# RWKV-7 recurrence with a GELU feed-forward layer: first loads in half transfers

## The chip, the cores and the metric

One core of a Trainium2 chip. The core has five engines that run side by side, each in the order of its own program: PE (matmuls), DVE (vector work), ACT (activations and copies), POOL (a slower vector engine) and SP, which here only issues DMA transfers. 16 DMA engines move the data. The metric is the device time of one execution in microseconds; before and after are compared by their medians.

## The reference

Inputs are r, k, v, w, a, b of shape batch 4, heads 8, 768 time steps, 40 per head, and two weights. Each head keeps a 40x40 state:

```python
for t in range(S):
    y[:, :, t] = einsum('bhd,bhde->bhe', r_t, state)
    Sa = einsum('bhde,bhe->bhd', state, a_t)
    state = state * w_t[:, :, None, :] - einsum('bhd,bhe->bhde', Sa, b_t) \
            + einsum('bhd,bhe->bhde', v_t, k_t)
...
x = y.transpose(0, 2, 1, 3).reshape(3072, 320)
h = x @ w_in                      # 320 x 2048
out = (0.5 * h * (1 + erf(h / sqrt(2)))) @ w_out
```

All inputs arrive at this kernel as written, and the two weights in 8-byte words (`wide_in`, `wide_out`), which the kernel has to turn to 4-byte floats itself.

## The kernel before

Time is cut into 12 chunks of 64 steps. In a chunk the recurrence is a set of small matmuls over 32 (batch, head) pairs. Its results go, 256 tokens at a time, through the feed-forward layer, one chunk behind.

Every piece of work is a named step, a small Python function. `order()` (line 19) is one long list of step names with their arguments, written out by hand; line 1436 performs them in that order. Each engine receives its instructions in the order in which the steps come, and does not reorder ACT, DVE, POOL or SP work. So a wait on ACT holds up everything that stands behind it on ACT. Waits are put in by the tile framework where a tile is read after it is written. Each DMA transfer has one of eight completion semaphores, taken in turn.

The steps that matter here, with their lines:

- Row loads, all issued by SP. `Lw.c` (472), `La.c` (483), `Lb.c` (490), `Lk.c` (494) and, for the first chunks, `Lr.c` (508) call `load_rows` (458), which brings chunk c of one input, 64 time steps by 16 (batch, head) rows of 40 floats for each half e of the partitions. Each run in memory is 160 bytes. From chunk 3 on, `Lw`, `La` and `Lr` load in another way (`load_pairs`, line 463, and line 479); `Lb` and `Lk` keep `load_rows`. `LV` (498) has its own code with the same shape, at line 500.
- Word loads. `Lf.kt.x.part` (544) brings 64 rows of words of w_in, each run 2 KB; where kt is 3 and x is 1 it takes 40 rows and 24 rows. `Lf5` (555) brings the last 16-row pieces (line 561), `Ls` (586) words of w_out (line 591).
- Their readers. `lg.c` (697, instructions at line 699) takes the logarithm of what `Lw.c` brought, on ACT. `ce.u` (621, lines 625 and 626) is the first step of turning unit u of words to floats, on ACT, followed by work on DVE. `ce.2` needs `Lf.2.0.0` and `Lf.2.1.0`; `ce.5` needs `Lf.0.0.1` and `Lf.0.1.1`; `ce.4` needs the `Lf5` words.
- The chain of chunk 0. `qm.k` (990) squares a 32x32 block matrix on PE, `qz.k` (1008) transposes on DVE, `qb.k.z` (1013) masks, one half on ACT (line 1016). Then `vm.0` (895), `jm.0` (1047) and `km.0` (1072) on PE, `jc.0` (1061, line 1065), `qx` (1034, line 1036), `xc0.0` (1135, line 1131) and `kt0.0` (1096, line 1090) on ACT.
- `warm` steps (449) are matmuls whose result nobody reads.

The part of the list around the first loads reads (cut):

```python
... Lw.0 pads_extra.0 Lb.0 ... La.0 ... Lw.1 ... Lf.0.0.0 ... Lf.0.1.0 ... Lb.1 ...
... Lf.1.0.0 ... Lf.2.0.0 ... Lf.1.1.0 ... La.1 ... Lf.3.0.0 ... Lk.0 Lf.3.1.0 ... Lf5.1.0 ...
... Lf.0.1.1 ... Lr.0 Lf.2.1.1 ... LV.0 ... Lf.2.1.0 ... Lf.2.0.1 ... Lk.1 ... Lf.0.0.1 Lw.2 ...
... Lb.2 ... La.2 ... Lf5.0.0 ... LV.1 Ls.4 ... Ls.0 ... Lf5.0.1 ... Lf5.1.1 ...
```

Of the kernel before, what the change touches and what calls it, by code (L numbers as in the profile page):

```python
# [114 lines left out]
def kernel(  # L115
# [13 lines left out]
    B, H, S, D = r.shape  # L129
# [4 lines left out]
    BL = 32  # L134
    NP = H // 2
    G = B // 2
# [10 lines left out]
    NB = 3  # L147
# [9 lines left out]
    def tile_of(name, shape, dtype=FP32):  # L157
        return const.tile(shape, dtype, name=name)
# [25 lines left out]
    def half(j, n=HP):  # L184
        return slice(j * HP, j * HP + n)
# [24 lines left out]
    part = tile_of("part", [P, G, DM])  # L210
# [112 lines left out]
    def engine(queue):  # L323
        return {"s": nc.sync, "a": nc.scalar, "p": nc.gpsimd}[queue]
# [131 lines left out]
    def rows_of(src, c, e):  # L456
        return src[G * e:G * (e + 1), :, c * C:(c + 1) * C, :].rearrange("g h t d -> t (g h) d")

    def load_rows(c, src, t, eng):
        for e in range(2):  # L460
            eng.dma_start(out=t[half(e)].rearrange("p g h d -> p (g h) d")[:, :, :D], in_=rows_of(src, c, e))

    def load_pairs(c, src, t, eng):
        rows = slice(c * C // 2, (c + 1) * C // 2)
# [6 lines left out]
    @step  # L471
    def Lw(c, q="s"):
        to = rows(w_of(c))
        if c < NB:
            load_rows(c, w, to, engine(q))
        else:
            for e in range(2):
                for g in range(G):
                    engine(q).dma_start(out=to[half(e ^ g), g],  # L479
                                        in_=w[G * e + g, :, c * C:(c + 1) * C].rearrange("h t d -> t h d"))  # L480

    @step
    def La(c, q="s"):
        if c < NT:
            load_rows(c, a, by_64(a_of(c)).rearrange("p (g h) d -> p g h d", g=G), engine(q))
        else:
            load_pairs(c, a, paired["a"], engine(q))

    @step
    def Lb(c, q="s"):  # L490
        load_rows(c, b, rows(b_of(c)), engine(q))
# [41 lines left out]
    def first_home(kt, part):  # L533
        if not wide_in:
            return w_in_sb[:, kt, part * LW // 2:(part + 1) * LW // 2]
        if part == 0:
            return flat_out[:, kt * LW:(kt + 1) * LW]
        return flat_xt[:, :LW] if kt == NK - 1 else flat_gt[:, kt * LW:(kt + 1) * LW]
# [4 lines left out]
    @step  # L543
    def Lf(kt, x, part, q="s"):
        words = first_home(kt, part).rearrange("p (b n) -> p b n", b=2)
        src = first_from.rearrange("r (j x n) -> x r j n", x=2, n=FW // 2)[x]
        at, row = x * HP, x * D + 2 * D * kt
        n = min(HP, DM - row)
        for to, begin, many in (at, row, n), (at + n, 0, HP - n):
            if many:  # L550
                engine(q).dma_start(out=words[to:to + many],
                                    in_=src[begin:begin + many, 2 * part:2 * part + 2])

    @step
    def Lf5(part, x, q="s"):
# [912 lines left out]
```

## Time and profile before

| what | value |
|---|---|
| median of 3 runs | 632.1 us (631.37 to 632.44) |
| the profiled execution | 632.67 us |
| its span, first to last instruction | 630.9 us |
| mean granted clock of PE | 0.995 |
| DMA moved | 63.97 MB in 246,550 packets, 101 GB/s |
| HBM read / written | 54.39 MB / 3.93 MB |

In a timeline row stand the start in us from the span's start, the duration, the engine and line, what is written and read, the number of merged instructions, and in brackets how long the engine was idle before and what ended that. `SPq` rows are SP's issues of DMA transfers: their duration is the time of issuing, not of the transfer. A row of a group of issues gives the shortest, median and longest duration in ns and the first and last start. A window row gives busy time and instructions of PE, PEld, DVE, ACT and POOL, then PE's granted clock, the DMA engines' busy share (packets overlap, so it can exceed 1) and GB/s.

### The profile page before, as it was taken

How to read it: one execution, taken by the hardware profiler on the slowest of the kernel's cores; microseconds unless marked ns; L12 is line 12 of the kernel's file. 1: busy time of each engine (PE TensorE's matmuls, PEld its weight loads, DVE VectorE, ACT ScalarE, POOL GpSimd, SP SyncE). 2: the span in 40 equal slices, each digit the busy share in tenths (PEclk: the TensorE clock that was granted, in tenths of full speed). 3: DMA queues.
4: the chain of work that ended last, by engine and by line, in shares of the span. 5: the costliest groups of instructions: out<-in, count | busy, mean ns of one | idle time of the engine just before them, and what ended most of it. 6: DMA issues, size and time to landing. Idle time of an engine off the chain costs nothing.

```text
span 630.9 us, 31485 instructions
## 1 busy us (share of the span) xinstructions
PE 619.7 (98%) x14196; PEld 521.8 (83%) x14196; DVE 454.4 (72%) x558; ACT 345.4 (55%) x475; POOL 369.6 (59%) x797
## 2 busy tenths in 40 slices
PE   8989999999999999999999999999999999999997
PEld 5777787777987987987987988987988978978977
DVE  1788998875979978996886785875867955744313
ACT  4866897685454637636654647445557435243020
POOL 6278565738814875868848818838813886830000
PEclk9998999999999999999999999999999999999999
DMA  9997887722555766665575554444663454110100
GB/s 153 166 155 166 188 181 175 132 62 47 117 109 86 146 116 119 128 124 102 98 133 101 108 108 87 83 77 96 123 132 51 85 87 86 34 25 4 43 3 21
DMA packets 246550, 63.97 MB, mean 101 GB/s; under 512 B 228216, under 2 KB 243328, under 8 KB 246416
## 3 DMA queue, kind: packets, MB, share of 16 engines
q1 hardware_dynamic: 245976, 61.68, 52.0%
q8 instruction: 111, 1.82, 1.2%
q10 hardware_dynamic: 440, 0.29, 0.2%
q14 instruction: 23, 0.19, 0.1%
HBM read 54.39 MB, written 3.93 MB: 92 GB/s over the span
## 4 chain that ended last, share of the span: by engine, by line
PE 95%; ACT 1%; DVE 1%; SPq 1%; issue 1%; DMA 0%; DVEq 0%; ACTq 0%
PE bank L1308 33%; PE bank L188 30%; PE bank L1347 27%; PE bank L1429 3%; PE bank L763 2%; SPq L479 0%; SPq L1226 0%; DMA xt<-xt 0%; ACT st L1016 0%; DVE os L1298 0%; ACT L727 0%; ACT N L918 0%; DVE N L876 0%; ACT kT L727 0%; ACT gt L1313 0%
## 5 line engine op out<-in xcount | busy, mean ns | idle before, releaser
L1308 PE MATMUL bank<-xt,w_in_sb 64*64 64x256 f32 x3840 | 220.5, 377 | 1.1 <-DMA xt<-xt 1.1
L957 POOL TENSOR_TENSOR tmp<-W,Nb 128x126 f32<-128x126 f32 (+22 forms) x341 | 156.9, 460 | 77.3 <-DVE Nb L923 51.7
L1308 PEld LDWEIGHTS bank<-xt,w_in_sb 64*64 64x64 f32 x3840 | 147.1, 133 | 52.1 <-issue 1.8
L959 POOL TENSOR_TENSOR W<-W,tmp 128x126 f32<-128x126 f32 (+22 forms) x341 | 163.7, 480 | 26.7
L1347 PE MATMUL bank<-w_out_sb,gt 128*128 128x160 f32 x704 | 102.0, 302 | 0.2 <-ACT gt L1313 0.2
L1347 PEld LDWEIGHTS bank<-w_out_sb,gt 128*128 128x128 f32 x704 | 96.6, 190 | 3.5 <-issue 1.3
L1313 ACT ACTIVATE gt<-bank 128x1024 f32<-128x1024 f32 x48 | 49.1, 1024 | 73.1 <-PE bank L1308 71.9
L1152 DVE TENSOR_TENSOR SM<-bank,upper 128x832 f32<-128x832 f32 (+1 forms) x24 | 22.9, 989 | 19.5 <-PE bank L188 19.4
L1262 ACT COPY conv<-st 32x128 f32<-32x128 f32 (+2 forms) x55 | 28.0, 510 | 14.5 <-DVE st L1256 13.7
L1298 DVE TENSOR_TENSOR os<-os,bank 128x160 f32<-128x160 f32 x44 | 14.0, 319 | 28.5 <-PE bank L1347 19.1
L1347 PE MATMUL bank<-extra,conv 128*128 128x160 f32 x208 | 30.0, 299 | 0.0
L1313 ACT ACT_TABLE_LOAD x23 | 29.5, 1283 | 0.4
L1298 DVE TENSOR_TENSOR conv<-gt 128x1024 f32<-128x1024 f32 x11 | 14.0, 1272 | 21.0 <-ACT gt L1313 21.0
L1347 PEld LDWEIGHTS bank<-extra,conv 128*128 128x128 f32 x208 | 28.9, 190 | 0.0
L1204 DVE TENSOR_TENSOR st<-bank,st 128x832 f32<-128x832 f32 (+1 forms) x22 | 21.2, 986 | 8.8 <-PE bank L188 8.8
L1347 PE MATMUL bank<-extra,gt 128*128 128x160 f32 x176 | 26.4, 303 | 0.2 <-DVE os L1298 0.2
L734 DVE TENSOR_TENSOR_SCAN kT<-spare,kT 128x256 f32<-128x256 f32 x36 | 26.1, 782 | 0.6 <-ACT kT L727 0.6
L1347 PEld LDWEIGHTS bank<-extra,gt 128*128 128x128 f32 x176 | 24.3, 190 | 1.5 <-issue 0.9
L942 POOL MEMSET W<- 128x512 f32 x11 | 5.8, 525 | 32.9 <-DVE Tt L928 32.9
L801 POOL TENSOR_TENSOR bk_rows<-bk_rows,part 128x640 f32<-128x640 f32 x9 | 14.5, 1614 | 14.1 <-DMA bk_rows<-in_k_dram 14.1
L699 ACT ACT_TABLE_LOAD x11 | 14.1, 1283 | 13.8 <-DMA w_tile<-in_w_dram 13.7
L754 ACT ACT_TABLE_LOAD x11 | 14.1, 1283 | 13.1 <-PE bank L188 12.7
(227 smaller groups left out, 1156.1 us busy)
## 6 DMA issues: line engine op xcount, KB each, us to landing
bk_rows<-in_b_dram SPq DMA_DIRECT2D x24, 160.0 KB
bk_rows<-in_k_dram SPq DMA_DIRECT2D x24, 160.0 KB
out_dram<-os SPq DMA_DIRECT2D x46, 80.0 KB
VR<-in_v_dram SPq DMA_DIRECT2D x22, 160.0 KB
w_tile<-in_w_dram SPq DMA_DIRECT2D x36, 80.0 KB
v_pairs<-in_w_dram SPq DMA_DIRECT2D x18, 144.0 KB
a_pairs<-in_a_dram SPq DMA_DIRECT2D x18, 144.0 KB
a_pairs<-in_b_dram SPq DMA_DIRECT2D x18, 144.0 KB
```

Of the source, the lines that this page charges most:

```text
L188: nc.tensor.matmul(o, lhsT, rhs, start=first, stop=True, skip_group_check=True)
L734: nc.vector.tensor_tensor_scan(logs[:, at:at + n], onward, logs[:, at:at + n], 0.0, ALU.mult, ALU.add)
L957: nc.gpsimd.tensor_tensor(t, W[:, BL // 2 - rows:, rest:rest + 1].to_broadcast([P, rows, rest]), Nb[:, rest:rest + 1, :rest].to_broadcast( ...
L959: nc.gpsimd.tensor_tensor(own, own, t, ALU.add)
L1152: nc.vector.tensor_tensor(SM[:, g, :, :, cols], pair_of(f"S{c}_", g).rearrange("p x i c -> p i x c")[:, :, :, cols], kept, ALU.mult)
L1204: nc.vector.tensor_tensor(to, pair_of(f"QY{c}_", g)[:, :, :, cols], to, ALU.add)
L1262: nc.scalar.copy(apart.rearrange("p e i g d -> p (e i g) d")[to_rows, :, to_col:to_col + n], st.rearrange("p e i g c -> p (e i g) c")[rows ...
L1298: nc.vector.tensor_tensor(to, one_, other, how)
L1308: nc.tensor.matmul(ph[half(x ^ y), x, s], w_in_sb[half(x), kt, at:at + HP], xt[half(x), kt], start=kt == 0, stop=kt == NK - 1, skip_group_ ...
L1313: nc.scalar.activation(gt[:, 4 * q:4 * q + 4].rearrange("p (x s) t -> p x s t", x=2), bank(f"ph{c}_{q}").rearrange("p x (s t) -> p x s t", ...
L1347: nc.tensor.matmul(po[:, n, :DM // 2], l_[:, f], r_[:, f], start=f == 0, stop=f == NF // 2 - 1)
L1429: nc.tensor.matmul(po[:, g, :DM], gt[:, f, g * P:(g + 1) * P], w_out_sb[:, f], start=f == 0, stop=f == NF - 1)
```

## The change

`load_rows` now cuts the transfer of each half e in two, 8 of the 16 (batch, head) rows each, if the chunk is one of the first three (`NB` is 3, `H` is 8, `G` is 2). From chunk 3 on it stays one transfer. `Lf` cuts every piece into parts of at most 32 rows (`BL` is 32): 64 rows become 32 and 32, 40 become 32 and 8, 24 stay. The steps, their list and every other instruction stay; `LV`, `Lf5`, `Ls` and the pair loads are untouched. What waits for a load now waits for all its parts.

```diff
     def load_rows(c, src, t, eng):
         for e in range(2):
-            eng.dma_start(out=t[half(e)].rearrange("p g h d -> p (g h) d")[:, :, :D], in_=rows_of(src, c, e))
+            to, words = t[half(e)].rearrange("p g h d -> p (g h) d")[:, :, :D], rows_of(src, c, e)
+            for n in range(0, G * H, H if c < NB else G * H):
+                some = slice(n, n + H if c < NB else G * H)
+                eng.dma_start(out=to[:, some], in_=words[:, some])
...
         for to, begin, many in (at, row, n), (at + n, 0, HP - n):
-            if many:
-                engine(q).dma_start(out=words[to:to + many],
-                                    in_=src[begin:begin + many, 2 * part:2 * part + 2])
+            for m in range(0, many, BL):
+                k = min(BL, many - m)
+                engine(q).dma_start(out=words[to + m:to + m + k],
+                                    in_=src[begin + m:begin + m + k, 2 * part:2 * part + 2])
```

## The prediction

> **What bounds the kernel now.** I read the page first (busy shares, slices, chain), then the timeline of SP's queue, the early timeline, and the windows.
>
> ```profile
> span 630.9 us, 31485 instructions
> PE 619.7 (98%) x14196; PEld 521.8 (83%) x14196; DVE 454.4 (72%) x558; ACT 345.4 (55%) x475; POOL 369.6 (59%) x797
> ...
> DMA  9997887722555766665575554444663454110100
> ...
> PE 95%; ACT 1%; DVE 1%; SPq 1%; issue 1%; DMA 0%; DVEq 0%; ACTq 0%
> ```
>
> PE is busy 98% and makes 95% of the chain that ended last: what PE loses early it has little idle time to win back. All changed transfers lie in the first 85 us of a 631 us span. There the DMA engines are full: the first three slices read 9.
>
> ```profile
> 4.00:8.00 4.00, 4.00 (x7) 1.61 (x6) 0.00 (x0) 2.70 (x3) 3.67 (x19) 1.00 1.12 171
> 16.00:20.00 4.00, 3.89 (x38) 2.78 (x38) 2.36 (x5) 3.37 (x6) 0.00 (x0) 1.00 1.15 199
> ```
>
> Last two columns: DMA share and GB/s. Row loads (160-byte runs) move at 171 GB/s, words (2 KB runs) at up to 199. Which loads matter shows in the waits, and in the rows right behind a load:
>
> ```profile
> 5.28 1.28 ACT L699 ACT_TABLE_LOAD   x1 [5.28 <-DMA w_tile<-in_w_dram]
> ...
> 38.72 0.77 ACT L625 ACTIVATE conv<-w_out_sb,rebias 128x512 int16<-128x512 int16 x1
> ...
> 39.40 0.77 ACT L626 ACTIVATE conv<-w_out_sb,rebias 128x512 int16<-128x512 int16 x1
> ...
> 40.21 0.72 ACT L1016 ACTIVATE st<-st,of_half 128x512 f32<-128x512 f32 x1
> ...
> 40.99 2.06 PE L188 MATMUL bank<-turned,st 64*64 64x32 f32 x64
> ...
> 46.12 1.28 ACT L699 ACT_TABLE_LOAD   x1 [1.48 <-DMA w_tile<-in_w_dram]
> ...
> 47.42 0.74 ACT L699 ACTIVATE w_tile<-w_tile 128x640 f32<-128x640 f32 x1
> ...
> 48.78 1.18 ACT L1065 COPY turned<-bank 32x512 f32<-32x512 f32 x2 [0.63 <-PE bank L188]
> ...
> 49.98 2.50 ACT L1036 COPY Tt<-turned 32x512 f32<-32x512 f32 x4
> ...
> 52.71 0.85 ACT L1131 COPY SM<-bank 128x832 f32<-128x832 f32 x1 [0.23 <-PE bank L188]
> ...
> 54.66 0.57 ACT L1090 COPY Tt<-bank 32x512 f32<-32x512 f32 x1 [1.09 <-DVE Tt L1090]
> ```
>
> Three places on ACT, which works strictly in its written order. Lw.0 is waited for at 5.28. At 38.72 ACT converts words of Lf.2.1.0 (step ce.2), and right behind it stand qb.3.1.a (40.21) and PE's qm.4 (40.99), which needs it: a microsecond lost at ce.2 is lost by PE. At 46.12 ACT waits 1.48 us for Lw.2, but behind it three waits on others (0.63, 0.23, 1.09) leave 1.95 us before step kt0 at 54.66 moves.
>
> **The change part by part.** It removes no work and moves no step: the same bytes go in more issues. 15 row loads (Lw, La, Lb, Lk, Lr of chunks 0 to 2) go from 2 transfers to 4, which adds 30. 14 word transfers of 64 rows become two of 32, the two of 40 rows become 32 and 8, those of 24 stay: 16 more. So 46 more issues on SP, all between 0.8 us and 85 us. What does one cost?
>
> ```profile
> L461 SPq DMA_DIRECT2D bk_rows<-in_b_dram x24: 595/674/2370, 2.3 to 506.5; - x24
> ...
> L479 SPq DMA_DIRECT2D w_tile<-in_w_dram x36: 595/633/1767, 107.9 to 533.3; - x36
> ...
> L551 SPq DMA_DIRECT2D w_out_sb<-in_moe_w_in_dram x9: 299/1091/2581, 8.2 to 32.6; - x9
> ...
> L469 SPq DMA_DIRECT2D v_pairs<-in_w_dram x36: 312/488/1699, 86.7 to 473.0; - x36
> ...
> L561 SPq DMA_DIRECT2D w_out_sb<-in_moe_w_in_dram x8: 422/444/2811, 46.6 to 56.6; - x8
> ```
>
> (ns, shortest/median/longest.) L479 is already the new row transfer's shape: 64 partitions of 8 heads of 40. It takes 0.633 us, and its shortest, 0.595, is that of L461 with 16 heads. So an issue costs the same for half the bytes. For 32 rows of words there is no row. Below it stands L561 (16 rows, 0.422), above it a 64-row one:
>
> ```profile
> 34.05 0.61 SPq L551 DMA_DIRECT2D gt<-in_moe_w_in_dram  x1
> ```
>
> I take L469's 0.488, since it too has 32 partitions, and keep 0.422 and 0.61 as bounds. Between issues lies 0.04 us (0.81+1.46 to 2.31):
>
> ```profile
> 0.81 1.46 SPq L461 DMA_DIRECT2D w_tile<-in_w_dram  x2
> 2.31 1.70 SPq L461 DMA_DIRECT2D bk_rows<-in_b_dram  x2
> ...
> 26.26 0.61 SPq L551 DMA_DIRECT2D gt<-in_moe_w_in_dram  x1
> 27.37 1.32 SPq L461 DMA_DIRECT2D r_pairs<-in_r_dram  x2
> ...
> 31.20 1.32 SPq L500 DMA_DIRECT2D VR<-in_v_dram  x2
> 32.57 1.44 SPq L551 DMA_DIRECT2D w_out_sb<-in_moe_w_in_dram  x1
> ...
> 39.92 1.31 SPq L461 DMA_DIRECT2D w_tile<-in_w_dram  x2
> ```
>
> A half row transfer is 82 KB, 0.48 us at 171 GB/s, against 0.67 us of SP: SP becomes slower than the engines on rows. A half word transfer is 131 KB, 0.66 us at 199 GB/s, against 0.53: there the engines still set the pace.
>
> The Trainium skill, DMA: Bandwidth & Descriptors, section Issuing engines are not separate DMA queues, says that the sequencer's time to initiate a DMA is usually small relative to the DMA. By that the change would cost nothing; the L479 row speaks against it here.
>
> Now SP's clock, unstalled. Up to the end of Lf.2.1.0: start 0.81; 8 row loads, 32 issues of 0.67, 21.5; words 9x2+3 = 21 of 0.53, 11.1; four L561 of 0.48, 1.9; one VR, 1.4; the 0.5 us hole before 27.37. Sum 37.2, against 32.57+1.44 = 34.0 before. From end of issue to landing: Lw.0 ended its issue at 2.27 and ended a wait at 5.28, 3.0 us with an almost empty queue; Lw.2, 41.23 to 46.12, 4.9 us with a full one. When SP is the slower side the queue is short, so I take 3.0: ce.2's words land at 40.2, against ACT's 38.72. That is **+1.5 us** at ce.2, and through qb.3.1.a at PE's qm.4. With 0.422 for the words it is 38.8, +0.1; with 0.61, 42.8, about +4.
>
> Lw.2: two more row loads and two word transfers in halves, SP ends at 37.2+5.4+2.1 = 44.7, landing 47.7, against 46.12: +1.6, inside the 1.95 us. Bounds: about 0 to +4.6, of which 2.6 would show.
>
> ```profile
> 6.83 1.26 PE L188 MATMUL bank<-cum_m,ident 128*128 128x512 f32 x2
> ```
>
> The start: four issues end at about 3.5 instead of 2.27, but the last transfer is half as long: Lw.0 lands 0.3 to 0.7 us later. PE works on warm-up matmuls until 6.83+1.26 = 8.1; I book +0.3 at PE. It lies inside the +1.5, which counts from a fixed time. Lf5 at 60.22:
>
> ```profile
> 55.15 1.88 SPq L561 DMA_DIRECT2D w_out_sb<-in_moe_w_in_dram  x4
> ...
> 60.22 0.78 ACT L625 ACTIVATE conv<-w_out_sb,rebias 128x512 int16<-128x512 int16 x1 [1.50 <-DMA w_out_sb<-in_moe_w_in_dram]
> ...
> 63.23 1.01 ACT L848 COPY late<-bank 128x1024 f32<-128x1024 f32 x1 [1.57 <-PE bank L188]
> ```
>
> Between Lw.2 and it SP has eight more row issues and 14 others, 12.7 us unstalled: 57.4, where it was 55.15+1.88 = 57.0, 3.2 us before the wait's end. It is hidden by ACT being 1.5 us late itself, and by the 1.57 us of the next wait. After that no load of the list is followed so closely. The extra completions (46 x 16 small writes) I leave at nothing: they go over 16 engines, 46 each.
>
> Sum: the profiled execution took 632.67 us (span 630.9); 632.67+1.5 = 634.2. The three runs have a median of 632.1, 0.6 lower, so **633.6 us**. The case's own range, from the bounds at ce.2, is 632.2 to 636.1.
>
> **The rivals.**
>
> *Faster: PE's fetch stall goes.* Price:
>
> ```profile
> 45.93 0.91 PE L188 MATMUL bank<-rT,late 40*64 40x64 f32 x20 [1.92 <-issue]
> ...
> 48.61 2.08 PE L188 MATMUL bank<-cum_m,ident 128*128 128x512 f32 x2
> ...
> 17.30 1.02 PE L188 MATMUL bank<-cum_m,ident 128*128 128x512 f32 x2
> ...
> 44.00:46.00 2.00, 0.08 (x5) 0.08 (x7) 1.90 (x3) 0.64 (x1) 1.76 (x4) 0.71 0.66 73
> 46.00:48.00 2.00, 2.00 (x66) 1.88 (x68) 0.66 (x2) 1.86 (x2) 1.69 (x5) 0.50 0.93 160
> ...
> q8 instruction: 111, 1.82, 1.2%
> ```
>
> In the middle of step vm.0 PE stands for 1.92 us and no semaphore ended it. The likely cause is its instructions: queue 8 brings them in pieces of 1.82 MB/111 = 16 KB over the same engines. Then the granted clock falls to 0.50, and the two matmuls of 1.02 us take 2.08. If SP's slower pace leaves the engines shorter queues, the piece comes in time, and both losses go. The gain is capped by ACT: from the end of Lw.2's logarithm (47.42+0.74 = 48.16) ACT has 1.18+2.50+0.85+0.57 = 5.1 us of its own to kt0's end, so kt0 could end at 53.3 instead of 55.2, 1.95 us earlier, if Lw.2 is not late: 632.1-1.95+0.3 = 630.4. For it: the stall is real and lies under a full DMA queue. Against it: Lw.2's lateness eats the gain one for one, and words still fill the engines. It decides when Lw.2 lands less than 0.4 us later. A weaker form only absorbs the +1.5 of ce.2 in the 1.92 us, about 632.5.
>
> The Trainium skill, TensorE: Matmul & The Clock Gate, section Part 1, says the gate looks at free-running windows of about 3.4 us. By that a stall of 1.92 us may or may not halve the clock, differently in each execution; here it did.
>
> *Hidden: the engines were the bound and stay it.* SP stalled inside many issues (1.44 at 32.57 where 0.61 would do), so its new work fills those stalls. This is the lower bound of my sum: 632.1 plus 0 to 0.5.
>
> *Slower still: 32 rows cost 0.61 us.* Then ce.2 is 4 us late, Lw.2 takes 2.6 past its slack, PE idles longer and the half clock comes again: 632.1+4 to 632.1+6, say 637. The same would come if the eight completion semaphores, taken in turn, make each issue wait for the eighth before it. At 4.9 us to landing that allows one in 0.61 us, just under SP's 0.67, so a longer landing decides.
>
> **How the numbers follow.** Forecast case 0.46, of which 0.08 lies within 0.2% (the absorbed form); hidden 0.14; slower still 0.20; faster 0.20. About 0.2% (1.3 us) is what a measurement can tell from no change. So faster 0.20, within 0.22, slower 0.58. The range reaches to the faster rival and the slower one's middle: 630.3 to 637.0.
>
> **What would show it.** Right: SP's row issues at 0.6 us without long ones in the first 40 us; a wait on DMA before ACT's L625 near 39 to 40 us, and PE's 64x32 group near 42.5 instead of 40.99; DMA share under 1.0 in 4:8. Hidden: the same landing times at 5.28 and 46.12, long issues still there. Faster: no idle of PE near 44 to 46 and a clock of 1.00 throughout. Wrong altogether: a difference that arises after 100 us, where no transfer changed.

## The result, and the profile after

The changed kernel takes 639.5 us (median of 4 runs, 638.2 to 641.84), the kernel before in the same comparison 632.3 (631.37 to 632.78). The ratio is 1.012, with a 95% interval of 1.0087 to 1.0153. The forecast was slower, at 633.6 with a range up to 637.0. The direction holds; the size is about five times what was forecast, and outside the range. (One of the ten later executions of the kernel before took 1611 us and is left out of its ratio below.)

The profiled execution took 640.12 us with a span of 638.4, 7.5 us more than before. From its page, the span, the busy time of PE, the DMA slices, and the chain of work that ended last:

```profile
span 638.4 us, 31566 instructions
...
PE 619.7 (97%) x14196; PEld 523.3 (82%) x14196; DVE 454.0 (71%) x558; ACT 344.8 (54%) x475; POOL 370.1 (58%) x797
...
DMA  6676688750647658646565755334754454110100
...
PE 80%; SPq 11%; DMA 3%; ACT 3%; issue 2%; DVE 1%; POOL 0%; DVEq 0%; ACTq 0%; POOLq 0%
```

PE is busy for the same 619.7 us, so all of the 7.5 us is waiting. The half clock (granted clock 0.50) lasts 6.83 us in both profiles, so it does not make the difference. The first slices of the DMA engines read 6 and 7 where they read 9, and SP's issuing has 11% of the chain where it had 1%. The windows say the same (the last two columns are DMA share and GB/s; before, they were 1.12 and 171, then 1.15 and 199):

```profile
4.00:8.00 4.00, 4.00 (x7) 1.59 (x6) 0.00 (x0) 2.29 (x3) 3.67 (x19) 1.00 0.74 116
16.00:20.00 4.00, 3.88 (x38) 2.78 (x38) 2.21 (x4) 3.44 (x6) 0.00 (x0) 1.00 0.51 98
```

The DMA engines are no longer full. SP is the slower side, as the forecast had it. This is SP's queue in the timeline (start, duration, and at the end the number of issues merged in a row):

```profile
9.08 2.67 SPq L464 DMA_DIRECT2D SM<-in_w_dram  x4
11.80 2.03 SPq L555 DMA_DIRECT2D w_out_sb<-in_moe_w_in_dram  x4
13.87 4.08 SPq L464 DMA_DIRECT2D bk_rows<-in_b_dram  x4
17.99 2.98 SPq L555 DMA_DIRECT2D w_out_sb<-in_moe_w_in_dram  x6
21.02 2.64 SPq L464 DMA_DIRECT2D spare<-in_a_dram  x4
23.70 1.79 SPq L555 DMA_DIRECT2D w_out_sb<-in_moe_w_in_dram  x2
...
29.65 3.11 SPq L565 DMA_DIRECT2D xt<-in_moe_w_in_dram  x4
...
39.69 1.30 SPq L555 DMA_DIRECT2D w_out_sb<-in_moe_w_in_dram  x2
...
47.14 2.66 SPq L464 DMA_DIRECT2D w_tile<-in_w_dram  x4
...
63.31 1.90 SPq L565 DMA_DIRECT2D w_out_sb<-in_moe_w_in_dram  x4
```

Four half rows take 2.67 us, 0.67 each, as forecast; six half words 2.98, 0.50 each. But now and then SP stalls, that is, a group takes about a microsecond more than its like: 4.08 at 13.87, 1.79 for two at 23.70, 3.11 at 29.65. So the words of ce.2 (39.69) are issued by 41.0 us, not 37.2 as the forecast's clock had it, Lw.2 (47.14) by 49.8, not 44.7, and Lf5.0.1 (63.31) by 65.2, not 57.4.

This is what it does to ACT, in the timeline (in brackets the idle time before, and what ended it):

```profile
44.23 0.77 ACT L629 ACTIVATE conv<-w_out_sb,rebias 128x512 int16<-128x512 int16 x1 [3.52 <-DMA w_out_sb<-in_moe_w_in_dram]
...
52.46 1.28 ACT L703 ACT_TABLE_LOAD   x1 [1.62 <-DMA w_tile<-in_w_dram]
...
69.25 0.77 ACT L629 ACTIVATE conv<-w_out_sb,rebias 128x512 int16<-128x512 int16 x1 [6.21 <-DMA xt<-in_moe_w_in_dram]
```

ce.2 starts at 44.23 instead of 38.72, the logarithm for Lw.2 (lg.2) at 52.46 instead of 46.12, ce.4 at 69.25 instead of 60.22. And this is what it does to PE; the second block has the same groups before, and one more at 50.61:

```profile
26.10 1.09 PE L767 MATMUL bank<-ident,spare 128*128 128x128 f32 x8 [1.49 <-DMA spare<-in_a_dram]
...
42.91 1.97 PE L188 MATMUL bank<-ident,VR 128*64 128x128 f32 x32 [1.87 <-DMA VR<-in_v_dram]
46.30 2.05 PE L188 MATMUL bank<-turned,st 64*64 64x32 f32 x62 [1.43 <-ACT st L1020]
...
59.61 1.66 PE L188 MATMUL bank<-SM,Tt 64*64 64x104 f32 x64 [1.12 <-ACT Tt L1094]
...
71.61 1.09 PE L767 MATMUL bank<-ident,a_pairs 128*128 128x128 f32 x8 [1.60 <-ACT late L852]
```

```profile
24.50 1.04 PE L763 MATMUL bank<-ident,spare 128*128 128x128 f32 x8
...
39.09 1.97 PE L188 MATMUL bank<-ident,VR 128*64 128x128 f32 x32
...
50.61 2.14 PE L188 MATMUL bank<-VR,nT 64*64 64x104 f32 x64
...
55.29 1.93 PE L188 MATMUL bank<-SM,Tt 64*64 64x104 f32 x64
...
65.79 1.04 PE L763 MATMUL bank<-ident,a_pairs 128*128 128x128 f32 x8
```

The five groups of the first block are the reader of La.1, the reader of LV.0, and the steps qm.4 and sm.0 (both chunk 0) and ta.2 (chunk 2). PE reaches them 1.6, 3.8, 5.3 (46.30 against 40.99), 4.3 and 5.8 us late. Between qm.4 and sm.0 it wins some back: the stop of 1.92 us in vm.0 is gone. The half clock is still there, from 48.1 us on instead of 44.8. So 5.8 of the 7.5 us are there by 72 us. (ACT's wait at 69.25 is for the words of Lf5.0.1, whose last piece lands at 69.07; the view names a load that came about the same time.)

### The profile page after: what moved, and what is told of

It reads as the page before. It is cut to its first block, busy times and chain, and to the rows that moved or that the text cites. A ratio compares the mean times of both kernels' runs of the same rounds, so it can differ in the third digit from the quotient of the medians.

```text
span 638.4 us, 31566 instructions
## 1 busy us (share of the span) xinstructions
PE 619.7 (97%) x14196; PEld 523.3 (82%) x14196; DVE 454.0 (71%) x558; ACT 344.8 (54%) x475; POOL 370.1 (58%) x797
## 4 chain that ended last, share of the span: by engine, by line
PE 80%; SPq 11%; DMA 3%; ACT 3%; issue 2%; DVE 1%; POOL 0%; DVEq 0%; ACTq 0%; POOLq 0%
PE bank L1312 32%; PE bank L1351 24%; PE bank L188 21%; SPq L464 4%; PE bank L1433 3%; SPq L555 2%; DMA w_out_sb<-in_moe_w_in_dram 1%; SPq L482 1%; SPq L565 1%; DMA xt<-xt 1%; SPq L1230 1%; SPq L503 1%; DMA v_pairs<-in_r_dram 0%; SPq L595 0%; DMA bk_rows<-in_k_dram 0%
## 5 line engine op out<-in xcount | busy, mean ns | idle before, releaser
L961 POOL TENSOR_TENSOR tmp<-W,Nb 128x126 f32<-128x126 f32 (+22 forms) x341 | 158.8, 466 | 76.5 <-DVE Nb L927 50.9
L1312 PEld LDWEIGHTS bank<-xt,w_in_sb 64*64 64x64 f32 x3840 | 148.8, 133 | 51.6 <-issue 3.3
L963 POOL TENSOR_TENSOR W<-W,tmp 128x126 f32<-128x126 f32 (+22 forms) x341 | 161.9, 475 | 26.7
L703 ACT ACT_TABLE_LOAD x11 | 14.1, 1283 | 15.6 <-DMA w_tile<-in_w_dram 15.4
L188 PEld LDWEIGHTS bank<-SM,Tt 64*64 64x64 f32 x768 | 18.4, 133 | 4.1 <-ACT Tt L1094 1.6
```

Of the source, the lines that this page charges most:

```text
L188: nc.tensor.matmul(o, lhsT, rhs, start=first, stop=True, skip_group_check=True)
L961: nc.gpsimd.tensor_tensor(t, W[:, BL // 2 - rows:, rest:rest + 1].to_broadcast([P, rows, rest]), Nb[:, rest:rest + 1, :rest].to_broadcast( ...
L963: nc.gpsimd.tensor_tensor(own, own, t, ALU.add)
L1312: nc.tensor.matmul(ph[half(x ^ y), x, s], w_in_sb[half(x), kt, at:at + HP], xt[half(x), kt], start=kt == 0, stop=kt == NK - 1, skip_group_ ...
```

## The experiments

Each comparison has its own runs of the kernel before; so the ratios are to be compared, not the microseconds (the medians of before lay between 632.3 and 635.5). "Lg.2" below is the start of ACT's table load for lg.2, the step that needs Lw.2, in the profile of that run.

**Which half of the change.** Rows alone, and words alone (part of the diff undone):

```diff
-            for m in range(0, many, BL):
-                k = min(BL, many - m)
+            for m in range(0, many, HP):
+                k = min(HP, many - m)
```

> Only the 15 row loads go in halves, the words stay whole. Theory 'issue' (what counts is the time that SP needs to issue, and loads that land after their reader is ready): a whole word transfer takes SP 0.61 us, its halves took 0.42 + 0.47 in the profile after, so some 2.5 us of SP time go by the end of Lf.2.1.0; its words land near 41.6 us instead of 44.11, and the loss of 7.3 us falls to 3 to 5: 635 to 637. Theory 'engines' (every smaller transfer costs the DMA engines a fixed amount, whatever its kind): 30 of the 46 new transfers are left, 30/46 of 7.3 us, 637. Alone this run does not tell the two apart; with the next one it does.

Ratio 1.0044 (1.0026 to 1.0063), lg.2 at 49.12. At the low end of what was expected.

```diff
-            for n in range(0, G * H, H if c < NB else G * H):
-                some = slice(n, n + H if c < NB else G * H)
+            for n in range(0, G * H, G * H):
+                some = slice(n, n + G * H)
```

> Only the words go in halves, the rows stay whole. 'Issue': 16 issues more at about 0.27 us each, some 4 us, against over 10 us that SP stood stalled inside issues in the first 40 us of before: hidden, 631.5 to 633. 'Engines': 16 of 46 new transfers, 2.5 us, 634.8.

Ratio 0.9972 (0.9954 to 0.9991), lg.2 at 45.41: 1.8 us faster than before, better than either theory had it. "Engines" falls here: by it the words' part costs 2.5 us.

> The words-only kernel once more, beside the others and for its interval. If it is really faster: -0.45 to -0.1%, and PE does not stand for want of instructions near 44 us. If the first interval was luck: -0.1 to +0.1%.

Once more: 0.9981 (0.9952 to 1.001), lg.2 at 45.80. Both intervals hold -0.2%; the second does not exclude no change. PE's timeline around the place of the stop, words alone:

```profile
42.00 2.06 PE L188 MATMUL bank<-turned,st 64*64 64x32 f32 x64
44.10 1.16 PE L188 MATMUL bank<-rT,late 40*64 40x64 f32 x64
46.31 1.20 PE L188 MATMUL bank<-st,N 32*32 32x32 f32 x64 [1.05 <-DVE st L1035]
47.44 1.13 PE L188 MATMUL bank<-cum_m,ident 128*128 128x512 f32 x2
```

vm.0's 64 matmuls run through in 1.16 us; the next wait is an ordinary one, on DVE.

**Is that stop in the kernel before, or in one execution of it?**

> The kernel before on this chip, for its trace. If PE's stop of 1.92 us at 44 us and the half clock behind it are part of the kernel and not of one execution, both are there again; if they come and go, the words-only gain is partly luck of the execution.

The ratio is 1.0009 (0.9986 to 1.0032), as it should be. The timeline of PE:

```profile
40.34 1.31 PE L188 MATMUL bank<-ident,VR 128*64 128x128 f32 x20 [0.80 <-issue]
...
45.54 0.56 PE L188 MATMUL bank<-rT,late 40*64 40x64 f32 x20 [0.95 <-issue]
```

The stop comes again, in two parts of 0.80 and 0.95 us, and the half clock follows it again (0.53 and 0.50 from 46 to 52 us). Neither of the two words-alone profiles has such a stop. Of the half clock the first has none, the second a piece of 3.41 us. But the stop is missing in the profile of the rows alone too (there PE waits 0.70 us for ACT, which is behind with ce.2, while the piece with its instructions comes), so its absence does not make a kernel faster by itself.

**Only the words in the middle.**

```diff
+        size = BL if kt in (0, 2) and (part or (kt, x) == (2, 1)) else HP
```

> Rows whole; of the words only those go in halves that SP issues between 26 and 40 us (Lf.0.1.1, Lf.2.1.1, Lf.2.1.0, Lf.2.0.1, Lf.0.0.1), 5 more issues. If the gain of the words-only run is that PE's instruction piece of 42.9 us gets through sooner, it is all here: -0.35 to -0.15%, with no idle of PE for want of instructions near 44 us. If it is spread over all the word loads: -0.1 to +0.1%.

Ratio 1.0004 (0.9979 to 1.0029). The stop is gone here too and lg.2 starts at 45.05, but the half clock is there for 6.83 us. So the gain of the words is not pinned to these five pieces, and the clock comes and goes with the execution.

The granted clock of every execution is on record, and it sorts these small differences. A half clock of 6.83 us makes a mean clock of 0.995. In all four sets of runs of the kernel before, the executions at 0.995 or less took 2.0 to 2.5 us more on average than those at 0.996 or more. Among the latter, words alone are only 0.6 and 0.5 us faster than before (0.1%), which the scatter does not tell from nothing; but 9 of 10 and 9 of 12 of their executions are among them, against 7 of 14 and 10 of 23 of the kernel before. So most of the gain of the words goes with a half clock that comes less often. The words in the middle gain nothing at either clock.

**Is it the number of issues or the size of a transfer?** Rows as 15 heads and 1 head:

```diff
+            cuts = (0, 15, 16) if c < NB else (0, 16)
+            for n, m in zip(cuts, cuts[1:]):
+                eng.dma_start(out=to[:, n:m], in_=words[:, n:m])
```

> Rows in two transfers of 15 heads and 1 head instead of 8 and 8, words whole. 'Issue': an issue costs the same whatever it moves, so the time is that of the rows-only run within 0.7 us. A form of 'engines' in which it is the halved size that moves slower: the 15-head transfer is nearly the whole one, so 633 to 634. If issuing costs by the amount of data instead of by the instruction, also 633 to 634.

Ratio 1.008 (1.0064 to 1.0097), lg.2 at 51.44. It is not the halved size: a transfer that is nearly whole does not help. It was expected within 0.7 us of the rows-only run and is 0.36%, 2.3 us, above it. Two groups that cost 2.65 and 2.64 us in the rows-only run (Lb.1, La.1) take 3.04 and 4.44 here; why is not settled.

Words in parts of 16 rows, rows whole (`BL // 2` for `BL` in `Lf`):

> Rows whole, words in parts of 16 rows instead of 32. An issue of 16 rows takes SP 0.42 us as one of 32 does, so a 64-row piece costs 1.85 us instead of 0.9: 9 us more up to the words of ce.2. 'Issue': the stalls that SP has left in the words-only run hold some 4 of them, the rest makes ce.2 late: 0 to +0.6%. If what helped in the words-only run is that shorter transfers let PE's instructions through sooner, and that is all that counts, it helps more here: -0.5 to -0.3%.

Ratio 1.0119 (1.0069 to 1.0168), lg.2 at 53.98: as slow as the whole change, without one row load in halves. It has 48 issues more than before, the whole change 46. The number of issues counts, of whatever kind. The expectation of at most +0.6% was a miss, of the same sort as the prediction: it let SP's stalls take up 4 of 9 us, but the words of ce.2 are issued by 42.4 us, 8.4 later than before.

**Where the rows count.** The whole change once more, then with chunk 2's rows whole (`c < 2` for `c < NB`), then with only chunk 2's in halves (`c == 2`):

> The changed kernel itself, so that the parts stand beside the whole on one chip. If the parts simply add up (rows +0.44%, words -0.28%), the whole is near +0.2%. 'Issue': SP can take up only so much in the stalls it has; the rows use that up and the words' 4 us then come on top in full: +0.9 to +1.3%, as first measured.

> The whole change, but the rows of chunk 2 go whole (10 of the 30 new row issues undone, all of them behind the words of ce.2). 'Issue': up to ce.2 all is as late as with the whole change (La.1 at 26.3 us, VR at 42.9, the words of ce.2 at 44.1); Lw.2 lands 1.3 us sooner than 52.2, still late by 4 to 5, and what follows (La.2, the Lf5 words) 4 us sooner: +0.6 to +0.9%. If the place didn't matter, two thirds of the rows' part, about the same as the whole change less 0.25%.

> The words in halves and of the rows only those of chunk 2. 'Issue': as the words-only run up to 39.5 us; then Lw.2 takes 1.3 us longer to issue, but in the words-only run it landed 1.8 us sooner than before, so its reader does not wait longer than before: -0.3 to +0.1%. If any halved row load costs the same, a third of the rows' part on top of the words: about 0.

Ratios 1.0108 (1.0051 to 1.0165), 1.0073 (1.0036 to 1.0109) and 1.0012 (0.9983 to 1.0042); lg.2 at 51.62, 52.59 and 47.27. The parts do not add up: rows +0.44, words -0.2 to -0.3, together +1.1%. That is the form of a budget: alone the words cost nothing since SP has time for them, beside the halved rows it has not. The other two runs do not tell "issue" from the reading in which the place of a halved load does not matter: 1.0073 and 1.0012 lie within or next to what either expected, and the intervals are wider than the distance between them. Lg.2, expected 1.3 us sooner in the second run than in the changed kernel, came no sooner.

**SP's time taken away, the halves kept.** ACT, idle until Lw.0 lands, issues the e = 1 halves of Lw.0, Lb.0 and La.0:

```diff
+                by = nc.scalar if c == 0 and e and (src is w or src is b or src is a) else eng
+                by.dma_start(out=to[:, some], in_=words[:, some])
```

> The whole change, but the two halves for e = 1 of Lw.0, Lb.0 and La.0 are issued by ACT, which is idle until Lw.0 lands: 6 issues, 4.1 us, leave SP's queue. 'Issue': every later load lands 4.1 us earlier until the DMA engines are full; of what was late (La.1 by 1.8, LV.0 by 3.8, the words of ce.2 by 5.3) at most 1.2 us is left: 632 to 634. 'Engines': the transfers are the same ones, so 639 to 640.

Ratio 1.0063 (1.0045 to 1.008), lg.2 at 49.58. About half of the loss is gone when 6 of the issues leave SP, with the same transfers, which "engines" forbids; but 632 to 634 was too hopeful.

POOL besides, idle from 12 to 27 us, issues 11 word transfers (`Lf.1.0.0` becomes `Lf.1.0.0.p`, and so on):

> The whole change with all its halves, but beside the 6 issues that ACT takes over, POOL (idle from 12 to 27 us) issues the 11 word transfers of Lf.1.0.0, Lf.2.0.0, Lf.1.1.0, Lf.3.0.0 and Lf.3.1.0. SP has some 5 us less to do before 30 us than in the two-queue run. If the loss is SP's time alone, ACT's logarithm for Lw.2 (46.1 us before, 49.6 in the two-queue run, 52.5 in the whole change) starts at 46 to 47.5 and the time is 0 to +0.3% over before. If halves cost something besides SP's time (on the DMA engines, in completions), it stays at +0.4 to +0.7% as with two queues.

Ratio 1.0066 (1.0044 to 1.0088), lg.2 at 48.65: no better, and outside what was expected. SP's queue of this run:

```profile
18.70 5.98 SPq L465 DMA_DIRECT2D bk_rows<-in_k_dram  x4
...
27.73 3.60 SPq L465 DMA_DIRECT2D r_pairs<-in_r_dram  x4
...
35.55 2.59 SPq L556 DMA_DIRECT2D gt<-in_moe_w_in_dram  x2
...
42.99 2.66 SPq L465 DMA_DIRECT2D w_tile<-in_w_dram  x4
```

Lr.0 starts at 27.73, where it started at 27.37 before: nearly all lateness is cured by then. More could not be won, since the DMA engines were full (share 1.13 and 1.08 from 16 to 24 us, and 5.98 us for four half rows). But from there to the end of Lw.2 SP takes 17.9 us (27.73 to 45.65) against 13.9 before (27.37 to 39.92+1.31 = 41.23): six row issues and four word issues more, and four stalls. So here what idle engines took over early did not help a load that comes late. PE is 2.5 us late at 100 us, 0.4%; the rest of the 0.66% arises later and is not explained.

With rows whole and the same POOL issues:

> Rows whole, words in halves, and the same 11 word transfers issued by POOL. If the words-only run gained because SP and the DMA engines run smoother, more of it: -0.5 to -0.2%. If the DMA engines are the bound there anyway, as in words-only: -0.3 to 0%. If POOL's issues are slow or late, ce.1 or the chunk 0 chain waits: above 0.

Ratio 1.0036 (1.0014 to 1.0058): slower, though lg.2 starts at 45.30 without a wait. Its profile has the half clock for 6.83 us, but that is not the reason: at 0.996 or more its executions are 2.0 us slower than those of the kernel before, and at 0.995 or less 2.1 us. Nor is it the first loads: PE is only 0.4 us late at 100 us. What it is stays open. Words alone, issued by SP, stays the best version found.

**Does ce.4's wait hold the loss?** Ls.4 and Ls.0 behind Lf5.0.1:

```diff
-LV.1 Ls.4 cs.7 cm.7 cv.7 pk.0 pb.0 od.0.1 Ls.0 om.0.0 sb.2 od.0.0 tv.1 wT.2 ic.1.8.12 Lf5.0.1 ce.4
+LV.1 cs.7 cm.7 cv.7 pk.0 pb.0 od.0.1 om.0.0 sb.2 od.0.0 tv.1 wT.2 ic.1.8.12 Lf5.0.1 Ls.4 Ls.0 ce.4
```

> The whole change, but the four issues of Ls.4 and Ls.0 (w_out's words, read only after 90 us) stand behind Lf5.0.1 in SP's order instead of ahead of it. If ce.4's wait for the Lf5 words (6.2 us on ACT in the profile after, and behind it PE's 1.6 us before ta.2) is what keeps the loss at the end, those words land 2.9 us sooner, ACT's wait is about 3.3 us, PE's gap before ta.2 is gone or under 0.4 us, and the time falls by 1 to 2.9 us: +0.75 to +1.05% over before. If the loss was made for good before 60 us, nothing changes: +1.1 to +1.2%.

Ratio 1.0109 (1.0069 to 1.0148): nothing gained that can be measured, though ACT's wait shrank more than expected, from 6.21 to 1.78 us. The interval still holds the 1.0075 to 1.0105 that the theory gave; what speaks against it is the trace. PE in that run:

```profile
55.23 0.24 PE L188 MATMUL bank<-turned 32*32 32x32 f32 x2 [2.26 <-ACT turned L1069]
...
57.68 2.50 PE L188 MATMUL bank<-w_tile,cum_m 128*128 128x320 f32 x4
60.11 2.78 PE L188 MATMUL bank<-SM,Tt 64*64 64x104 f32 x64
...
71.46 1.04 PE L767 MATMUL bank<-ident,a_pairs 128*128 128x128 f32 x8
```

The wait before ta.2 is gone, and ta.2 is no earlier (71.46, 71.61 in the first profile). PE had lost the time at 55.23, behind lg.2 on ACT, and to a half clock right after it (2.50 and 2.78 us for what took 1.34 and 1.66). The first profile has its half clock earlier, so the two are not quite alike. But the second profile of the whole change has it in the same place. There (55.3 to 62.2 us, against 55.6 to 62.5 in the Lf5 run) ACT waits 5.55 us at ce.4, and PE has no wait before ta.2 either (two rows of PE, then one of ACT, then PE's ta.2):

```profile
50.34 1.66 PE L188 MATMUL bank<-VR,nT 64*64 64x104 f32 x64
54.31 0.24 PE L188 MATMUL bank<-turned 32*32 32x32 f32 x2 [2.31 <-ACT turned L1069]
...
68.05 0.79 ACT L629 ACTIVATE conv<-w_out_sb,rebias 128x512 int16<-128x512 int16 x1 [5.55 <-DMA xt<-in_moe_w_in_dram]
...
70.66 1.04 PE L767 MATMUL bank<-ident,a_pairs 128*128 128x128 f32 x8
```

So the largest wait does not hold the loss: a wait of 5.55 us on ACT cost PE nothing at ta.2. This profile shows besides where the loss is made. At 50.34 PE is 0.3 us ahead of the kernel before (50.61); then it waits 2.31 us for jc.0, which stands behind lg.2 on ACT, and the half clock comes.

**Do early waits count, and where do SP's long issues come from?** One warm-up matmul of 512 columns becomes 64 of 32x32:

```diff
-        for n in range(3):
+        for n in range(2):
             mm(pt[:, n % 2], w_in_sb[:, 0, :P], w_in_sb[:, 0, :512])
+        for n in range(H * H):
+            mm(pt[:BL, 1, :BL], w_in_sb[:BL, 0, :BL], w_in_sb[:BL, 0, :BL])
```

> The whole change, with one warm-up matmul of 512 columns replaced by 64 of 32x32 in the idle time at the start: some 126 PE instructions more ahead of everything, about half of a 16 KB piece, so queue 8 brings its pieces 2 to 4 us earlier than at 15.4, 23.3, 30.2, 36.8 and 44.7 us. If SP stalls because of these pieces, its issues of over 0.9 us move with them and each of them overlaps a piece; if they come from the order of the loads (a certain transfer, a turn of the semaphores), they stay at the same loads: Lb.1's third issue near 15.2, Lf.3.0.0 at 23.7, Lf5.1.0 near 30.1. The time is that of the whole change within 0.3% either way.

Ratio 1.0108 (1.0073 to 1.0144), lg.2 at 52.13. SP's queue of this run:

```profile
14.39 2.64 SPq L466 DMA_DIRECT2D bk_rows<-in_b_dram  x4
...
20.09 3.70 SPq L466 DMA_DIRECT2D spare<-in_a_dram  x4
...
29.08 2.33 SPq L567 DMA_DIRECT2D xt<-in_moe_w_in_dram  x4
```

The same loads in the changed kernel: 4.08, 2.64 and 3.11. Lb.1 has lost its stall, La.1 has got one. The pieces of PE's instructions have moved too, though not by half a piece and earlier, as expected. The trace has 126 matmuls more, not 63, and with their weight loads that is one piece more (112 instead of 111, the new one at 9.6 us). So the others come at the same places of PE's program, which PE reaches later: at 22.1, 28.7, 34.5 and 43.2 us instead of 15.4, 23.3, 30.2 and 36.8. In the DMA view the changed kernel has one from 15.4 to 16.85 us, under Lb.1,

```profile
q8 instruction: 1, 0.02, 6.3%
```

and this run has one from 22 to 23.8 us, under La.1, and none from 14 to 21.9:

```profile
q8 instruction: 1, 0.02, 4.5%
```

Taking every SP issue of over 0.9 us in the first 100 us of the changed kernel and laying it beside the 16 KB packets of queue 8, all 14 overlap one, though the 14 pieces fill only 16 of the 100 us. In this run, to 70 us, it is 9 of 10; in the two-queue run, to 70 us, 9 of 9; in the kernel before, where full engines stall SP as well, 15 of 26 to 100 us. The ends agree even better: 13 of the 14 issues end 0.36 to 0.44 us after the piece, and the 9 of this run 0.38 to 0.50.

The same run shows something that was not asked. The first warm-up step, with the small matmuls in it, now lasts to 9.96 us instead of 7.04, and a half clock comes on top (8.95 to 15.78 us): the first matmuls on aT and nT start at 19.83, 5.8 us later than in the changed kernel (14.00). Yet the time is that of the whole change: PE, over 5 us late here, waits less for the loads that come later.

**All runs on one scale.** The table has the start of lg.2, the start of a group of PE's matmuls (on `turned` and `spare`) that comes at 99.53 us in the kernel before, when the loads that were cut are behind it, and the ratio:

| run | lg.2 (us) | PE's group (us) | ratio |
|---|---|---|---|
| words in the middle | 45.05 | 99.42 | 1.0004 |
| words, POOL | 45.30 | 99.89 | 1.0036 |
| words alone | 45.41 and 45.80 | 97.20 and 98.06 | 0.9972 and 0.9981 |
| before | 46.12 and 45.88 | 99.53 and 99.71 | 1 and 1.0009 |
| words, rows of chunk 2 | 47.27 | 100.61 | 1.0012 |
| three queues | 48.65 | 102.06 | 1.0066 |
| rows alone | 49.12 | 103.12 | 1.0044 |
| two queues | 49.58 | 103.73 | 1.0063 |
| 15 and 1 heads | 51.44 | 105.17 | 1.0080 |
| whole change | 52.46 and 51.62 | 106.45 and 105.27 | 1.0120 and 1.0108 |
| shifted instructions | 52.13 | 107.20 | 1.0108 |
| Lf5 first | 52.55 | 106.37 | 1.0109 |
| rows of chunks 0 and 1, words | 52.59 | 105.30 | 1.0073 |
| words of 16 rows | 53.98 | 106.74 | 1.0119 |

A later lg.2 goes with a longer time, about 1.1 us at the end for each microsecond (6.3 and 7.2 us for the whole change). PE's lateness at 100 us goes with it more closely. The change in time (the ratio less 1, times 632 us) is within 1.2 us of that lateness in all runs but the two in which POOL issues words, which lose 1.6 and 1.9 us more. So nearly all of the loss is made in the first 100 us. These are profiles of single executions, and it is not shown that lg.2 itself is the gate and not another load of the same time in SP's queue. PE's wait behind lg.2, in the second profile of the whole change and in the Lf5 run, speaks for it. An early delay of 5.8 us (shift) adds nothing to the time, and ce.4's wait holds at most a small part of the loss.

## Why the prediction was right or wrong

*SP becomes the slower side; a half row costs it a whole issue.* Right: 0.67 us each, DMA share 0.74 in 4 to 8 us.

*A half word transfer at 0.488 us.* Right on the mean, 0.50, but not because of the partitions: an issue of 32 rows is 0.42 us, as one of 16, and the first behind a row load 0.62.

*3.0 us from end of issue to landing.* Right: ce.2's words 41.0 to 44.2, Lw.2 49.8 to 52.46.

*SP's clock, unstalled.* This step failed, and with it every lateness worked out from it. The sum took every issue at its undisturbed length and so said that stalls go away once SP sets the pace. Those that came from full engines did go; those that lie on PE's instruction pieces stayed, about one in each 7 us, 0.6 to 1.4 us each. Counted as each long issue less its like, four of them make 4.2 us up to Lf.2.1.0, where the clock was 3.8 us too early, and eight make 7.3 us up to Lf5.0.1, where it was 7.8. The profile of the kernel before had both, the 111 pieces of queue 8 and the long issues of SP, and the prediction used the pieces only for PE's stop.

*ce.2 late by 1.5 us, and no more.* ce.2's start came 5.5 us late, and PE's qm.4 5.3 us. The bounds of that term reached to +4, by a 32-row issue of 0.61, which was the wrong reason.

*Lw.2's +1.6 lies inside the slack of 1.95.* The slack was read rightly: lg.2 is 6.3 us late and sm.0 4.3, that is 6.3 less 2.0. It is the lateness that was too small by 4.7, beyond its bound of +4.6, and with it the choice of the term: this one was booked at nothing, and it is the one that lasts. In the second profile of the whole change PE had won back all of ce.2's lateness by 50.34 us, and lost 2.31 us again behind lg.2.

*Hidden behind it: Lf5.* Wrong by the same clock; ACT waited 6.2 us at ce.4, and PE 1.60 at ta.2 in the first profile. The Lf5 run and the second profile show that it costs little or nothing of its own.

*Where to look.* La.1 and VR were not looked at, though by the forecast's own clock La.1 would land at about 25.2, after its reader at 24.50. PE did wait for both. The shifted run, in which PE is later than that by itself, shows that it did not matter.

*+0.3 at the start.* Not there: the matmuls that read Lw.0 start at 7.85 us, where they started at 7.93.

*Rival: PE's stop goes.* The mechanism is real. In the changed kernel the stop is absorbed: the piece (44.7 to 46.1 us) now comes while PE waits for ce.2. With the words alone it comes earlier (40.9 to 41.8, against 42.9 to 44.4 before), the stop is gone without such a wait, and the kernel is 0.2 to 0.3% faster, though the second interval does not exclude no change. The rival was tied to the whole change; it belongs to one half of it.

*Rival: hidden.* True for the words in halves of 32 rows, false with the rows.

*Rival: slower still, 637.* Nearest in size, with the wrong price behind it. The other price named there, eight completion semaphores in turn, is not needed: half rows went out at 0.67 us for whole stretches.

*The Trainium skill, DMA: Bandwidth & Descriptors, section Issuing engines are not separate DMA queues.* By its sentence that the initiating time is usually small the change would cost nothing. The trace disagrees: 0.67 us of issuing decided, against 0.48 of moving by the prediction's estimate.

*Wrong altogether: a difference after 100 us.* Not so; 6.9 of 7.5 us are there by vm.1 (90.13 against 83.24), and 5.7 of 7.0 in the second profile.

## What to carry to other kernels

Before a transfer is cut, compare its time on the engines with the time of its issue: here 0.48 us against 0.67 turned a queue bound by the DMA engines into one bound by the issuing engine, while cuts that stay above the issue time (0.66 against 0.50) cost nothing, and perhaps gained a little. Parts of 16 rows fall below it again (by estimate 66 KB at 199 GB/s, 0.33 us, against 0.42), and they cost 1.2%. When you forecast such a queue, keep the stalls that have another cause than the one you remove; find each long issue's companion in the trace first. The largest wait is not the costliest one: shrinking a wait of 6.2 us to 1.8 gave nothing that could be measured, and 5.8 us lost early cost nothing. And before a difference of 0.3% is explained, sort the executions by their granted clock.

## What the hardware showed that was not expected

SP's issue of a transfer lasts until PE's instruction piece is through: 14 of 14 long issues lie on one of the 16 KB packets of queue 8, 13 of them end 0.36 to 0.44 us after it, and when the pieces come at other times, the stalls come at other loads. That speaks for the pieces as the cause; by which path is open. An issue of 16, or of 32, rows of words costs SP 0.42 us and one of 64 rows 0.61, while a row load of 64 partitions takes 0.60 to 0.67 whether it brings 1, 8, 15 or 16 heads. PE's stop for instructions came in both executions of the kernel before that were profiled (1.92 us; 0.80 and 0.95 us) and in no profile of any changed kernel, with the words halved or only the rows.
